# GateLoop attention and a gated feed-forward on one core: the results of two chunks in one group of quadrant matmuls

## The chip, the cores and the metric

One core of a Trainium2 chip. The metric is the device time of one execution in microseconds (us). Five engines work beside each other, each through its own instructions in program order: PE (TensorE, the matmuls; its weight loads are shown apart as PEld), DVE (VectorE), ACT (ScalarE), POOL (GpSimd) and SP (SyncE, which here only issues DMAs). Where one engine needs another's result, it waits on a semaphore.

## The reference

```python
# q, k, v, a_re, a_im: (B, H, S, D) = (4, 8, 768, 48)
mag = sqrt(a_re * a_re + a_im * a_im)
scale = minimum(mag, 0.999) / (mag + 1e-06)
a_re_n, a_im_n = a_re * scale, a_im * scale
for t in range(S):                       # S_re, S_im: (B, H, D, D), start at 0
    ar, ai = a_re_n[:, :, t, :, None], a_im_n[:, :, t, :, None]
    new_re = ar * S_re - ai * S_im
    new_im = ar * S_im + ai * S_re
    S_re, S_im = new_re + einsum('bhd,bhe->bhde', k[:, :, t], v[:, :, t]), new_im
    y[:, :, t] = einsum('bhd,bhde->bhe', q[:, :, t], S_re)
x = y.transpose(0, 2, 1, 3).reshape(3072, 384)
h = x @ w_in                             # w_in: (384, 2048)
g = h * erf(maximum(h, 0) + log1p(exp(-abs(h))))
out = g @ w_out                          # w_out: (2048, 384)
```

All of it is float32.

## The kernel before

**Units and chunks.** The 4 x 768 tokens are worked in 12 units of 256 tokens, three to a sequence, and each unit in two chunks of 128 tokens. A name such as 3.1 is unit 3, chunk 1. Instead of stepping through tokens, a chunk uses products of decays: keys and queries are scaled and turned by the running product of the complex gates, so that within a chunk the results are a masked product of queries, keys and values, and what came before the chunk is one state S per head. Real and imaginary parts stand side by side, so a head's key has 96 elements.

**The steps of a unit**, with the letters that the order below uses: gates are loaded (`g`, L803) and worked into angles and decays by ACT and DVE, with a running sum over tokens as a matmul (`m t o l r s a`, and `p`, whose sum is at L1040). k and q are loaded (`k`, `q`, L807) and v (`v`, L814). `K` and `Q` (`prep`) are each a DVE multiplication by the decay (L1064, kr or qr, in a small buffer named "part"), one by the turn (L1069, kt or qt) and, from unit 2 on, a DVE transpose of 32 x 32 blocks (L1075, into X). `M` (`move`) then puts the blocks in their places with 12 DMAs in four pieces (L1086), so that KQ holds keys and queries with the 96 elements on the partitions: 16 planes of 128 tokens, eight heads of keys and then eight of queries. Units 0 and 1 do this with matmuls and copies instead (`kT`, `qT`, L1093 and L1097). `A` (`scores`) makes for four heads at once the products of keys and queries (L1106, sc) and, on DVE, masks them (L1110, A). `S` (`state`) makes kv from keys and values (L1125), adds the old state (L1131, Skv) and scales (L1134). It writes the one of two state buffers that the chunk before last used. `Y` (`result`) makes a chunk's results. ACT copies them into xT (L1163).

**The quadrant matmuls.** The results of a chunk, transposed, are 384 x 128. `result` makes them in blocks of 32 output rows, with weights of 128 x 32 (values, times A) and 96 x 32 (state, times queries). Four blocks for four different quadrants of TensorE's columns are issued in turn. A chunk has 64 such matmuls, or 32 where there is no state yet (the first chunk of a sequence). In the profile they are the `y` rows of L1161. All other matmuls have 96 or 128 weight columns.

**The feed-forward.** `h` makes h from xT and w_in (L1174, hps, 12 matmuls with 256 columns a piece) and ACT copies it (L1177). `x` is the softplus on ACT (names z and yy), `e` is ACT's error function (e<-z) between four DVE operations (L1203 to L1209). `O` is the product with w_out: L1243 in units 0 to 2, and from unit 3 on seven products of halves instead of eight (L1267, results W, X, Y, Z, with sums of h and of the weights made by DVE, `f` and `b`). `u` steps at the start are matmuls that nobody reads, issued to keep PE busy (L1325, unread). `n`, `i` and `Z` load and look over the weights.

**Buffers.** Of PSUM, ps_b with two buffers is shared by the decay sums, kv and y; ps_a holds the scores, ps_h the hps and ps_o the results of `O`. KQ has one buffer, A two, "part" two, and k and q one each, for both chunks of a unit.

**The order.** Every step is a generator. A string, `ORDER`, written out by hand, names the steps one after another, and each name runs the step to its next `yield`. So `Y2.0` stands twice: its first place issues all matmuls of the group, its second the copy. The string therefore fixes what stands behind what in every engine's queue, SP's too, and where in PE's work each group comes. Activations whose functions lie in different tables have a table load between them on ACT (L787), so their number too follows from the order.

Of the kernel before, what the change touches and what calls it, by code (L numbers as in the profile page):

```python
# [10 lines left out]
FP = mybir.dt.float32  # L11
# [9 lines left out]
P = 128  # L21
# [28 lines left out]
u8_0 u4_38 u4_21 u4_20 u4_2 g0.0 u2_34 u2_41 u2_25 g0.0 g0.1 g0.1 H t0.0 t0.0 m0.0 m0.0 m0.0 m0.1 t0.0 m0.1 l0.0  # L50
l0.0 t0.1 l0.0 l0.0 m0.1 l0.0 t0.1 t0.1 p0.0 u8_1 n0 n0 l0.1 o0.1 l0.1 l0.1 l0.1 o0.0 l0.1 n0 n0 k0.0 q0.0 p0.0
p0.0 K0.0 u2_23 r0.0 a0.0 r0.1 a0.0 a0.0 Q0.0 p0.1 u2_22 a0.1 u2_40 u2_39 g1.0 n1 m1.0 n1 n1 s0.0 s0.0 s0.0 Q0.0
qT0.0.0 p0.1 q0.1 a0.1 t1.0 p0.1 p0.0 K0.0 kT0.0.0 kT0.0.1 qT0.0.1 Q0.1 a0.1 t1.0 qT0.0.0 s0.1 s0.1 s0.1 qT0.0.1
g1.0 kT0.0.0 k0.1 u2_24 v0.0 S0.0 n1 K0.1 kT0.0.1 t1.0 o1.0 r1.0 A0.0.0 A0.0.0 Q0.1 K0.1 p0.0 S0.0 A0.0.1 A0.0.1
n3 n3 g1.1 m1.0 m1.1 t1.1 g1.1 a1.0 m1.0 a1.0 t1.1 a1.0 t1.1 qT0.1.0 qT0.1.0 v0.1 S0.1 S0.1 p0.1 l1.0 n4 n2 m1.1
m1.1 l1.0 g2.0 g2.0 p0.1 kT0.1.1 kT0.1.1 qT0.1.1 qT0.1.1 l1.0 o1.1 l1.0 n3 l1.0 Y0.0 kT0.1.0 A0.1.1 A0.1.1
kT0.1.0 A0.1.0 A0.1.0 l1.1 Y0.0 l1.1 s1.0 l1.1 n3 p1.0 p1.0 q1.0 l1.1 n2 l1.1 n2 g2.1 g2.1 p1.0 p1.0 n5 n6 r1.1
Y0.1 v2.1 k1.0 Y0.1 Q1.0 n2 n4 n4 n4 s1.0 s1.0 Q1.0 p1.1 a1.1 t2 m2 m2 m2 h0.0.6 t2 t2 S0.1 o2 n6 n6 p1.1 h0.0.6
l2 a1.1 a1.1 l2 p1.1 l2 l2 l2 K1.0 K1.0 n7 p1.1 q1.1 n6 k1.1 K1.1 Q1.1 g3.1 h0.0.4 h0.0.4 v1.0 a2.0 r2 a2.0 n7
n7 n7 n5 n5 qT1.0.1 qT1.0.0 h0.0.0 qT1.0.1 h0.0.0 s1.1 qT1.0.0 h0.0.2 h0.0.2 s1.1 s1.1 p2.0 p2.0 kT1.0.1 h0.1.0  # L60
kT1.0.1 kT1.0.0 a2.0 h0.1.0 kT1.0.0 p2.0 x0.0 a2.0 x0.0 e0.0.0 e0.0.2 A1.0.1 A1.0.1 A1.0.0 n5 n8 A1.0.0 n8 a2.0
# [12 lines left out]
e0.1.6 e0.1.4 n13 g5.0 a4.1 K3.0 n14 a4.1 e0.1.4 n14 e0.1.6 n14 x1.0 h1.1.4 x1.0 O0.8 h2.1.2 p4.1 O0.9 h2.0.2
O0.11 p4.1 x1.0 p4.1 x1.0 S3.0 S3.0 K3.1 g5.1 g5.1 M3.0 M3.0 M3.0 M3.0 e1.0.0 e1.0.0 e1.0.0 e1.0.2 e1.0.2 h2.0.2
e1.0.0 e1.0.2 e1.0.0 e1.0.2 e1.0.2 h2.1.2 m5 m5 a4.1 a4.1 j m5 O0.13 O0.15 O0.15 e1.0.4 h2.0.6 h2.0.6 e1.0.6
e1.0.6 e1.0.4 e1.0.4 e1.0.4 a4.1 e1.0.6 e1.0.6 e1.0.4 h2.1.4 A3.0.1 K3.1 A3.0.1 Q3.1 e1.0.6 Q3.1 v3.1 A3.0.0 l5
O0.10 A3.0.0 t5 l5 t5 x1.1 l5 l5 x1.1 S3.1 O0.12 O0.14 O0.14 x1.1 h2.0.4 O1.1 O1.3 h2.1.4 Y3.0 t5 S3.1 l5 o5
S3.1 x1.1 l5 l5 e1.1.2 e1.1.0 e1.1.2 e1.1.2 e1.1.2 e1.1.0 e1.1.0 e1.1.2 s4 s4 s4 r5 k4.0 K4.0 e1.1.0 e1.1.0 K4.0
e1.1.6 e1.1.6 e1.1.4 e1.1.4 e1.1.6 e1.1.4 e1.1.6 e1.1.6 O1.5 h2.0.0 O1.0 O1.2 M3.1 M3.1 M3.1 M3.1 A3.1.0 A3.1.0  # L80
A3.1.1 A3.1.1 O1.7 e1.1.4 K4.0 q4.0 Q4.0 k4.1 K4.1 e1.1.4 h2.0.0 h2.0.4 x2.0 Y3.0 x2.0 x2.0 x2.0 v4.0 p4.1 a5.0
p4.0 h2.1.6 O1.9 O1.11 S4.0 Y3.1 h2.1.0 O0.14 a5.0 K4.1 Q4.0 Q4.0 S4.0 q4.1 Q4.1 e2.0.0 e2.0.0 e2.0.0 e2.0.2
e2.0.2 e2.0.2 e2.0.0 e2.0.0 e2.0.2 p5.1 p5.1 h2.1.0 p5.1 e2.0.2 e2.0.6 Y3.1 h2.1.6 e2.0.6 e2.0.6 e2.0.4 a5.0
a5.0 e2.0.4 e2.0.4 O1.4 O1.6 O1.8 O1.13 O1.10 p5.0 p5.0 a5.0 a5.0 a5.0 x2.1 p5.0 x2.1 e2.0.4 e2.0.6 e2.0.6
h3.0.2 p4.0 M4.0 M4.0 M4.0 q5.1 M4.0 O0.15 k5.0 g6.1 p5.0 a5.1 g6.0 a5.1 a5.1 a5.1 x2.1 t6 x2.1 A4.0.1 A4.0.1
S4.1 S4.0 A4.0.0 A4.0.0 K4.1 S4.1 Q4.1 e2.0.4 Q4.1 e2.1.2 e2.1.2 e2.1.2 h3.0.4 h3.0.4 a5.1 O1.12 e2.1.0 e2.1.0
e2.1.2 a5.1 a5.1 e2.1.0 e2.1.2 e2.1.0 e2.1.0 p4.1 k5.1 g6.0 g6.1 h3.0.2 Y4.0 Y4.0 O1.14 O1.14 m6 m6 s5 e2.1.4
O1.15 O1.15 e2.1.6 e2.1.4 e2.1.6 e2.1.4 e2.1.6 h3.0.0 h3.0.0 s5 s5 e2.1.4 e2.1.4 S4.1 m6 e2.1.6 e2.1.6 h3.0.6
h3.0.6 M4.1 M4.1 M4.1 M4.1 h3.1.0 x3.0 t6 h3.1.0 x3.0 l6 x3.0 l6 x3.0 A4.1.1 h3.1.4 O2.1 O2.3 l6 K5.0 K5.0 q5.0
Q5.0 Q5.0 e3.0.0 Q5.0 v5.0 h3.1.6 A4.1.0 S5.0 t6 Q5.1 K5.1 A4.1.1 Q5.1 A4.1.0 Y4.1 K5.0 o6 S5.0 e3.0.0 e3.0.2  # L90
e3.0.0 e3.0.0 e3.0.2 e3.0.2 e3.0.0 e3.0.2 h3.1.4 r6 l6 O2.5 O2.7 a6.0 e3.0.6 a6.0 l6 e3.0.2 h3.1.2 O2.0 h3.1.2
h3.1.6 O2.9 e3.0.4 e3.0.6 e3.0.6 e3.0.4 a6.0 a6.0 O2.2 M5.0 a6.0 e3.0.4 M5.0 M5.0 M5.0 O2.4 O2.6 A5.0.0 A5.0.1
l6 l6 a6.1 p5.0 v6.0 q6.0 e3.0.6 e3.0.6 b2 e3.0.4 x3.1 Y4.1 h4.0.0 x3.1 a6.1 a6.1 x3.1 A5.0.0 A5.0.1 a6.1 a6.1
Y5.0 a6.1 b0 x3.1 O1.14 K5.1 K5.1 S5.0 a6.1 e3.0.4 Y5.0 f3.0 b4 Q5.1 e3.1.0 e3.1.0 e3.1.0 e3.1.0 e3.1.0 e3.1.2
e3.1.2 e3.1.2 e3.1.2 e3.1.2 k6.0 v6.1 O2.11 O2.13 p6.0 p6.0 p6.0 h4.0.0 p6.1 p6.1 e3.1.6 e3.1.6 h4.0.2 h4.0.2
e3.1.4 Q6.0 e3.1.4 O1.15 e3.1.4 e3.1.6 g7.0 g7.0 g7.1 p6.1 K6.0 f3.0 g7.1 m7 m7 M5.1 m7 e3.1.6 e3.1.4 e3.1.6
M5.1 i0 k6.1 i1 p6.0 q6.1 p6.1 M5.1 M5.1 O2.15 h4.0.4 h4.0.4 t7 O2.8 O2.10 O2.15 t7 l7 O2.12 O2.14 O2.14 O2.15
O2.14 b2 b2 t7 b0 b0 i0 l7 s6 l7 l7 b4 l7 b6 b2 e3.1.4 i1 f3.1 b6 b6 b4 h4.0.6 h4.0.6 x4.0 x4.0 b4 f3.1 l7 l7
x4.0 h4.1.0 O3.0 h4.1.0 x4.0 e4.0.0 a7.0 b6 O3.1 e4.0.2 h4.1.6 h4.1.6 o7 O3.1 r7 s6 A5.1.1 A5.1.1 O3.2 O3.2
e4.0.0 e4.0.2 e4.0.0 e4.0.2 e4.0.0 e4.0.2 e4.0.2 b0 e4.0.0 A5.1.0 s6 e4.0.4 e4.0.6 A5.1.0 a7.0 a7.0 e4.0.4  # L100
e4.0.4 e4.0.6 e4.0.6 h4.1.4 h4.1.4 O3.3 O3.4 h4.1.2 O3.5 v5.1 Y5.1 O3.6 O3.7 h4.1.2 x4.1 Y5.1 x4.1 a7.0 e4.0.4
Q6.0 Q6.0 K6.1 e4.0.6 O3.5 O3.5 K6.0 K6.0 O3.5 e4.0.4 Q6.1 O3.4 O3.7 O3.7 p6.1 M6.0 M6.0 e4.0.6 a7.0 a7.0 a7.0
x4.1 x4.1 e4.1.0 e4.1.0 e4.1.0 e4.1.2 p7.1 h5.0.2 h5.0.4 O3.8 O3.9 O3.12 p7.0 O3.10 O3.13 O3.11 p7.1 h5.0.2 p7.1
e4.1.2 e4.1.0 e4.1.2 e4.1.0 e4.1.2 e4.1.2 e4.1.6 e4.1.4 e4.1.6 e4.1.6 e4.1.4 e4.1.4 M6.0 M6.0 a7.1 g8.1 p6.0
a7.1 e4.1.6 e4.1.4 p7.0 h5.0.4 p7.0 a7.1 O3.13 e4.1.6 a7.1 f4.0 e4.1.4 f4.1 O3.11 S6.0 h5.0.6 g8.0 t8 t8 h5.0.6
m8 h5.0.0 Q6.1 i2 i2 A6.0.1 a7.1 a7.1 f4.1 a7.1 S6.0 q7.1 p7.0 i3 A6.0.1 O4.0 O4.1 A6.0.0 O4.2 O4.1 i3 O3.11
h5.0.0 A6.0.0 g8.0 O4.3 p7.1 g8.1 q7.0 O3.13 f4.0 O4.2 t8 o8 Q6.1 K6.1 K6.1 M6.1 M6.1 M6.1 x5.0 x5.0 x5.0 m8
x5.0 O4.4 O4.4 e5.0.2 e5.0.0 e5.0.2 e5.0.0 Q7.0 e5.0.2 e5.0.2 e5.0.0 m8 e5.0.0 e5.0.2 e5.0.0 h5.1.6 h5.1.6 s7 s7
s7 Q7.0 h5.1.2 h5.1.2 e5.0.6 e5.0.6 e5.0.4 e5.0.4 S6.1 e5.0.4 l8 M6.1 v7.0 O4.5 O4.5 S6.1 e5.0.6 h5.1.0 h5.1.4
# [1342 lines left out]
```

## Time and profile before

| | |
|---|---|
| median of 3 runs | 659.39 us (659.02 to 659.49) |
| the profiled execution | 659.63 us |
| its span, first to last instruction | 657.9 us |
| granted TensorE clock, mean | 0.997 |
| y matmuls, values times A (L1161) | 768, 33.5 us busy |
| y matmuls, state times queries (L1161) | 640 |
| hps matmuls (L1174) | 1152, 260.7 us busy |
| DVE masks (L1110) | 48, 31.9 us busy |

The span is cut into engines' busy time, and the rows of the profile give groups of equal instructions: the busy time of the group, the mean length of one, and the idle time of the engine just before them with what ended it. Matmuls are pipelined: a row's length of one is longer than the time from one start to the next, so busy times of groups overlap. "PE y L1161" is TensorE's work at line 1161 on the tile y; "A <- B: 2.0, 3, 0.9" in the list of waits says that A waited for B 2.0 us in all, three times, 0.9 us at most.

### The profile page before, as it was taken

How to read it: one execution, taken by the hardware profiler on the slowest of the kernel's cores; microseconds unless marked ns; L12 is line 12 of the kernel's file. 1: busy time of each engine (PE TensorE's matmuls, PEld its weight loads, DVE VectorE, ACT ScalarE, POOL GpSimd, SP SyncE). 2: the span in 40 equal slices, each digit the busy share in tenths (PEclk: the TensorE clock that was granted, in tenths of full speed). 3: DMA queues.
4: the chain of work that ended last, by engine and by line, in shares of the span. 5: the costliest groups of instructions: out<-in, count | busy, mean ns of one | idle time of the engine just before them, and what ended most of it. 6: DMA issues, size and time to landing. Idle time of an engine off the chain costs nothing.

```text
span 657.9 us, 12296 instructions
## 1 busy us (share of the span) xinstructions
PE 642.2 (98%) x4728; PEld 562.6 (86%) x4728; DVE 599.2 (91%) x976; ACT 581.7 (88%) x765; POOL 1.1 (0%) x8
## 2 busy tenths in 40 slices
PE   8999999999999999999999999999999999999995
PEld 7778887777777778989999998999998999999985
DVE  6999999999979899999999899899999998877883
ACT  6999999999999999998998999998996894788730
POOL 0000000000000000000000000000000000000000
PEclk9999999999999999999999999999999999999998
DMA  8896886536254358137448525626626507410020
GB/s 212 221 239 160 191 205 111 119 63 108 37 110 73 49 117 188 22 48 193 73 73 193 97 43 141 120 50 145 121 49 122 132 14 187 90 25 24 1 73 27
DMA packets 282792, 70.19 MB, mean 107 GB/s; under 512 B 269396, under 2 KB 272488, under 8 KB 282728
## 3 DMA queue, kind: packets, MB, share of 16 engines
q1 hardware_dynamic: 282728, 69.36, 49.0%
q8 instruction: 38, 0.62, 0.4%
q14 instruction: 26, 0.21, 0.1%
HBM read 48.82 MB, written 4.75 MB: 81 GB/s over the span
## 4 chain that ended last, share of the span: by engine, by line
PE 48%; ACT 30%; DVE 15%; DMA 3%; issue 3%; SPq 1%; POOL 0%; DVEq 0%; POOLq 0%; ACTq 0%
PE hps L1174 21%; ACT L787 7%; ACT yy L788 5%; ACT z L788 5%; PE Y L1267 4%; PE Z L1267 4%; PE X L1267 3%; PE y L1161 3%; PE sc L1106 3%; ACT e L788 3%; DVE z L1203 3%; DVE yy L1205 3%; DVE e L1207 2%; PE W L1267 2%; PE kv L1125 2%
## 5 line engine op out<-in xcount | busy, mean ns | idle before, releaser
L1174 PE MATMUL hps<-xT,w_in_sb 128*128 128x256 f32 x1152 | 260.7, 380 | 0.4 <-ACT xT L1163 0.3
L1174 PEld LDWEIGHTS hps<-xT,w_in_sb 128*128 128x128 f32 x1152 | 216.1, 190 | 32.6 <-ACT h L1177 1.4
L787 ACT ACT_TABLE_LOAD x95 | 121.9, 1283 | 2.4 <-PEq L1436 0.9
L1203 DVE TENSOR_TENSOR z<-z,yy 128x512 f32<-128x512 f32 x96 | 64.5, 687 | 18.6 <-ACT e L788 18.0
L788 ACT ACTIVATE e<-z 128x512 f32<-128x512 f32 x96 | 57.8, 627 | 21.1 <-DVE h L1209 20.6
L1209 DVE SCALAR_TENSOR_TENSOR h<-e,h 128x512 f32<-128x512 f32 x96 | 65.0, 685 | 1.3
L1243 PE MATMUL ops<-w_out_sb,h 128*128 128x384 f32 x192 | 66.2, 488 | 0.0
L1205 DVE SCALAR_TENSOR_TENSOR yy<-z,yy 128x512 f32<-128x512 f32 x96 | 64.6, 688 | 1.6
L1207 DVE TENSOR_TENSOR e<-e,yy 128x512 f32<-128x512 f32 x96 | 64.6, 685 | 0.9
L1177 ACT COPY h<-hps 128x512 f32<-128x512 f32 x96 | 54.5, 577 | 8.4 <-PE hps L1174 8.3
L1243 PEld LDWEIGHTS ops<-w_out_sb,h 128*128 128x128 f32 x192 | 35.8, 190 | 21.7 <-issue 0.8
L1106 PEld LDWEIGHTS sc<-KQ 96*128 96x128 f32 x384 | 47.0, 192 | 4.7 <-ACT KQ L1097 1.8
L1106 PE MATMUL sc<-KQ 96*128 96x128 f32 x384 | 49.0, 277 | 1.3 <-ACT KQ L1097 1.0
L788 ACT ACTIVATE yy<-z 128x2048 f32<-128x2048 f32 (+1 forms) x25 | 46.1, 1842 | 0.8 <-DVE found L859 0.4
L788 ACT ACTIVATE z<-h 128x2048 f32<-128x2048 f32 (+1 forms) x25 | 46.1, 1844 | 0.6 <-ACT h L1177 0.3
L788 ACT ACTIVATE z<-z 128x2048 f32<-128x2048 f32 (+1 forms) x25 | 46.1, 1845 | 0.5
L788 ACT ACTIVATE yy<-yy 128x2048 f32<-128x2048 f32 (+1 forms) x25 | 46.0, 1842 | 0.3
L1161 PE MATMUL y<-A,v 128*32 128x128 f32 x768 | 33.5, 275 | 0.9 <-DVE Skv L1131 0.6
L1110 DVE TENSOR_TENSOR A<-sc,triu 128x512 f32<-128x512 f32 x48 | 31.9, 679 | 1.8 <-PE sc L1106 1.8
L1125 PEld LDWEIGHTS kv<-v,kt 128*96 128x96 f32 x320 | 29.8, 165 | 1.6 <-issue 0.7
L1125 PE MATMUL kv<-v,kt 128*96 128x48 f32 x320 | 29.8, 246 | 0.0
L1267 PE MATMUL Y<-T,S 128*128 128x192 f32 x144 | 26.5, 331 | 1.5 <-DVE out L1275 1.1
(122 smaller groups left out, 1054.7 us busy)
## 6 DMA issues: line engine op xcount, KB each, us to landing
KQ<-X SPq DMA_DIRECT2D x240, 64.0 KB
raw<-in_moe_w_in_dram SPq DMA_DIRECT2D x8, 768.0 KB
raw<-in_moe_w_out_dram SPq DMA_DIRECT2D x8, 768.0 KB
again<-in_moe_w_in_dram SPq DMA_DIRECT2D x8, 768.0 KB
ar<-in_a_re_dram SPq DMA_DIRECT2D x24, 192.0 KB
ai<-in_a_im_dram SPq DMA_DIRECT2D x24, 192.0 KB
k<-in_k_dram SPq DMA_DIRECT2D x24, 192.0 KB
q<-in_q_dram SPq DMA_DIRECT2D x24, 192.0 KB
```

The source lines that it names most:

```text
L787: scalar.preload_act_table_set(sets[0])
L788: scalar.activation(func=func, **kw)
L1106: nc.tensor.matmul(out=ps[:, j, :], lhsT=head("k", g * HG + j, u, c), rhs=head("q", g * HG + j, u, c), start=True, stop=True)
L1125: nc.tensor.matmul(out=kv[0:D2, j, :], lhsT=T["kt", u, c][:, j].rearrange("p u d -> p (u d)"), rhs=side(T["v", u][:, c, j // 2], j % 2), s ...
L1174: nc.tensor.matmul(out=ps[:, e, :], lhsT=w_in_sb[:, (sl * SLAB + i) // 2, kd, e * P:(e + 1) * P], rhs=T["xT", u][:, kd, :], start=(kd == 0 ...
L1177: scalar.copy(out=T["h", u, sl][:, i:i + 2, :], in_=ps)
L1203: vector.tensor_tensor(out=z, in0=z, in1=y, op=OP.mult)
L1205: vector.scalar_tensor_tensor(out=y, in0=z, scalar=-2.0, in1=y, op0=OP.add, op1=OP.mult)
L1207: vector.tensor_tensor(out=e, in0=e, in1=y, op=OP.mult)
L1209: vector.scalar_tensor_tensor(out=h, in0=e, scalar=1.0 / RT2, in1=h, op0=OP.add, op1=OP.mult)
L1243: nc.tensor.matmul(out=ps, lhsT=lhsT, rhs=w_out_sb[:, i, :], start=i == HALF, stop=i == KF - 1)
L1267: nc.tensor.matmul(out=ps, lhsT=a(sl)[:, i], rhs=b(sl, i), start=sl == 0 and i == 0, stop=sl == NSL - 1 and i == HALF - 1)
```

## The change

From unit 2 on (`APART`) `result` takes both chunks of a unit: one step `Y2` to `Y11` issues the 64 (or 32) matmuls of chunk 0 and then the 64 of chunk 1, into two tiles of ps_b, and its next two places make the two copies. Units 0 and 1 keep a step for each chunk. KQ has two buffers instead of one, and the masked scores are written over the key half of the chunk's KQ, four heads after the first or the last four scores are made, so the tile A goes. k and q are loaded into a tile for each chunk, one buffer each, where before the one buffer held both chunks of a unit. "part" has one buffer. And the string `ORDER` is another one: the same steps with the same number of places, but for the joined `Y` steps and the `u` steps at the start, stand in other places throughout.

The code:

```diff
@@ -804,7 +803,8 @@
             yield
 
     def load(nm, src, u, c):
-        nc.sync.dma_start(out=whole(ldq, nm, u, [P, C, H, D])[:, c], in_=rows(src, u, c))
+        t = T[nm, u, c] = ldq.tile([P, H, D], FP, tag=nm, name=nm)
+        nc.sync.dma_start(out=t, in_=rows(src, u, c))
         yield
 
     def load_v(u, c):
@@ -1060,8 +1060,8 @@
 
 
     def prep(nm, u, c):
-        a = att1.tile([P, H, D], FP, tag="part", name=nm + "r", bufs=2)
-        vector.tensor_tensor(out=a, in0=T[nm, u][:, c], op=OP.mult,
+        a = att1.tile([P, H, D], FP, tag="part", name=nm + "r")
+        vector.tensor_tensor(out=a, in0=T[nm, u, c], op=OP.mult,
                              in1=T["pr", u][:, c, "qk".index(nm), :].rearrange("p (h d) -> p h d", d=D))
         yield
         t = T[nm + "t", u, c] = att1.tile([P, H, 2, D], FP, tag=nm + "t", name=nm + "t")
@@ -1076,7 +1076,7 @@
             yield
 
     def columns(u, c):
-        return whole(att2, "KQ", (u, c), [P, 2 * H, P], bufs=1)
+        return whole(att2, "KQ", (u, c), [P, 2 * H, P])
 
     def move(u, c):
         kq, x = columns(u, c), T["X", (u, c)]
@@ -1106,7 +1106,7 @@
             nc.tensor.matmul(out=ps[:, j, :], lhsT=head("k", g * HG + j, u, c), rhs=head("q", g * HG + j, u, c),
                              start=True, stop=True)
         yield
-        A = T["A", u, c, g] = att2.tile([P, HG, P], FP, tag="A", name="A")
+        A = T["A", u, c, g] = columns(u, c)[:, g * HG:(g + 1) * HG]
         vector.tensor_tensor(out=A, in0=ps, in1=triu.unsqueeze(1).to_broadcast([P, HG, P]), op=OP.mult)
         yield
 
@@ -1127,41 +1127,45 @@
         yield
         t = kv[0:D2]
         if not first:
-            t = att1.tile([P, H, D], FP, tag="part", name="Skv", bufs=2)[0:D2]
+            t = att1.tile([P, H, D], FP, tag="part", name="Skv")[0:D2]
             vector.tensor_tensor(out=paired(t), in0=paired(kv[0:D2]), in1=sides(sbuf[(u * C + c - 1) % 2]), op=OP.add)
             yield
         w = T["w", u, c][0:D2].unsqueeze(2).to_broadcast([D2, H, D])
         vector.tensor_tensor(out=sides(sbuf[(u * C + c) % 2]), in0=paired(t), in1=paired(w), op=OP.mult)
         yield
 
-    def result(u, c):
-
-        first = u % PER == 0 and c == 0
-        S = sbuf[(u * C + c - 1) % 2]
+    def result(u, chunks):
+
         x = whole(xp, "xT", u, [P, KD, NT])
-        ps = ps_b.tile([P, KD, P], FP, tag="b", name="y")
-
-        steps = [[] for _ in range(P // QUAD)]
-        for i in range(KD):
-            for b in range(P // QUAD):
-                pair, o = divmod((i * P + b * QUAD) // QUAD, 2 * D // QUAD)
-
-                parts = [(0, o * QUAD)] if o * QUAD < D else []
-                parts += [(1, o * QUAD + GAP)] if (o + 1) * QUAD > D else []
-                todo = []
-                for e, lo in parts:
-                    g, k_ = divmod(2 * pair + e, HG)
-                    both = [(T["v", u][:, c, pair, lo:lo + QUAD], T["A", u, c, g][:, k_, :])]
-                    if not first:
-                        both.append((S[0:D2, pair, lo:lo + QUAD], head("q", 2 * pair + e, u, c)))
-                    todo += both[::-1] if (len(steps[b]) + len(todo)) % 4 else both
-                steps[b] += [(i, lhsT, rhs, n == 0, n == len(todo) - 1) for n, (lhsT, rhs) in enumerate(todo)]
-        for turn in zip(*steps):
-            for b, (i, lhsT, rhs, start, stop) in enumerate(turn):
-                nc.tensor.matmul(out=ps[b * QUAD:(b + 1) * QUAD, i, :], lhsT=lhsT, rhs=rhs, start=start, stop=stop)
-        yield
-        scalar.copy(out=x[:, :, c * P:(c + 1) * P], in_=ps)
-        yield
+        out = []
+        for c in chunks:
+            first = u % PER == 0 and c == 0
+            S = sbuf[(u * C + c - 1) % 2]
+            ps = ps_b.tile([P, KD, P], FP, tag="b", name="y")
+            out.append((c, ps))
+
+            steps = [[] for _ in range(P // QUAD)]
+            for i in range(KD):
+                for b in range(P // QUAD):
+                    pair, o = divmod((i * P + b * QUAD) // QUAD, 2 * D // QUAD)
+
+                    parts = [(0, o * QUAD)] if o * QUAD < D else []
+                    parts += [(1, o * QUAD + GAP)] if (o + 1) * QUAD > D else []
+                    todo = []
+                    for e, lo in parts:
+                        g, k_ = divmod(2 * pair + e, HG)
+                        both = [(T["v", u][:, c, pair, lo:lo + QUAD], T["A", u, c, g][:, k_, :])]
+                        if not first:
+                            both.append((S[0:D2, pair, lo:lo + QUAD], head("q", 2 * pair + e, u, c)))
+                        todo += both[::-1] if (len(steps[b]) + len(todo)) % 4 else both
+                    steps[b] += [(i, lhsT, rhs, n == 0, n == len(todo) - 1) for n, (lhsT, rhs) in enumerate(todo)]
+            for turn in zip(*steps):
+                for b, (i, lhsT, rhs, start, stop) in enumerate(turn):
+                    nc.tensor.matmul(out=ps[b * QUAD:(b + 1) * QUAD, i, :], lhsT=lhsT, rhs=rhs, start=start, stop=stop)
+        yield
+        for c, ps in out:
+            scalar.copy(out=x[:, :, c * P:(c + 1) * P], in_=ps)
+            yield
 
 
     def ff_in(u, sl, i):
@@ -1222,7 +1226,7 @@
         vector.tensor_tensor(out=A21, in0=A11, in1=A21, op=OP.subtract)
         yield
 
-    PLAIN = 3
+    PLAIN, APART = 3, 2
     T["T4"] = const.tile([P, HALF, HD], FP, name="T4")
 
     def bank(u, nm):
@@ -1352,6 +1356,8 @@
         steps[f"b{r}"] = sums_of_weights(r, 2)
     for u in range(NU):
         plain = u < PLAIN
+        for nm, chunks in [(f"{u}.{c}", [c]) for c in range(C)] if u < APART else [(f"{u}", range(C))]:
+            steps["Y" + nm] = result(u, chunks)
         for c in range(C):
             at = f"{u}.{c}"
             steps["g" + at] = load_gates(u, c)
@@ -1367,7 +1373,6 @@
                 steps["S" + at] = state(u, c)
             for g in range(NHG):
                 steps[f"A{at}.{g}"] = scores(u, c, g)
-            steps["Y" + at] = result(u, c)
             steps["a" + at], steps["p" + at] = g_angle(u, c), g_decay(u, c)
         for at, cc in [(f"{u}.{c}", (c, c + 1)) for c in range(C)] if u < 2 else [(f"{u}", ALL)]:
             for nm, f in (("m", g_mag), ("t", g_tan), ("o", g_off), ("l", g_log), ("r", g_turn), ("s", g_sin)):
```

`ORDER` is replaced as a whole. The places around the results of unit 2 (a line "..." leaves out the rest):

```diff
-e0.0.6 e0.0.4 e0.0.6 m4 e0.0.6 e0.0.4 n15 k3.1 h1.0.4 h1.0.4 s3 h1.0.6 h1.0.6 Y2.0 p2.0 q3.0 p3.1 n12 e0.0.6
-S2.0 n12 M2.1 M2.1 M2.1 M2.1 n13 p3.0 v3.0 s3 p3.0 p3.1 s3 l4 x0.1 Y2.0 l4 x0.1 l4 x0.1 h1.1.6 h1.1.6 x0.1
...
-A2.1.0 A2.1.0 A2.1.1 A2.1.1 l4 e0.1.2 e0.1.0 e0.1.2 e0.1.0 h1.1.4 e0.1.2 e0.1.0 e0.1.2 e0.1.0 a4.0 a4.0 n14 Y2.1
-v4.1 Y2.1 g5.0 e0.1.6 e0.1.6 e0.1.6 e0.1.4 e0.1.4 e0.1.4 n13 Q3.0 n13 p4.0 O0.5 O0.7 p4.0 a4.0 a4.0 p4.0 a4.0
...
+A2.0.1 t4 n15 l4 O0.1 O0.0 O0.2 O0.4 O0.6 O0.3 A2.1.0 A2.1.0 A2.1.1 A2.1.1 e0.1.2 o4 l4 K3.0 e0.1.2 e0.1.0
+e0.1.0 h1.0.6 r4 h1.1.4 h1.1.4 e0.1.2 Y2 Y2 Y2 a4.0 v3.0 e0.1.0 e0.1.2 a4.0 e0.1.0 e0.1.2 e0.1.0 e0.1.6 e0.1.6
```

## The prediction, made before the changed kernel was run

> **What bounds it now.** I read the busy table first, then the same table by stretches of 100 us (the columns after each window: its length, PE, PEld, DVE, ACT and POOL busy, the granted clock, DMA's share, GB/s), then the list of waits, the costliest groups, and last the TensorE rows around one result group.
>
> ```profile
> PE 642.2 (98%) x4728; PEld 562.6 (86%) x4728; DVE 599.2 (91%) x976; ACT 581.7 (88%) x765; POOL 1.1 (0%) x8
> ```
>
> ```profile
> 0.00:100.00 100.00, 95.53 (x813) 81.32 (x814) 92.98 (x159) 93.82 (x159) 1.09 (x8) 1.00 0.84 203
> ...
> 200.00:300.00 100.00, 98.69 (x660) 83.10 (x659) 95.18 (x153) 98.81 (x126) 0.00 (x0) 1.00 0.43 83
> ...
> 500.00:600.00 100.00, 100.00 (x787) 92.63 (x786) 88.29 (x143) 76.02 (x92) 0.00 (x0) 1.00 0.39 87
> ```
>
> PE is busy all the time, so only what PE does, or how long it is idle, can move the end. But up to 300 us ACT is as full as PE (98.81 against 98.69), and DVE is near. From 400 on ACT has room. Work taken from PE early can therefore turn into waiting for ACT; taken late it should be won. The clock is 1.00, so time is not lost there.
>
> "Busy" overlaps, so I work with pitches, start to start: an hps matmul 216 ns, a product of ff_out 162, scores 112, kv 85, y 27. By them PE's work adds up to some 640 us and its true idle time to some 11: about 7 in the first 40 us, 1.0 at 182, 0.8 at 193, 1.1 at 281, small ones, and 2.6 behind 630.
>
> **The term that the change aims at.** Before, each of the 24 result groups stands alone between full-size matmuls. TensorE's rows around one (start, length, what, count):
>
> ```profile
> 487.23 1.46 PE L1267 MATMUL W<-w_out_sb,h 128*128 128x192 f32 x8
> 488.62 0.43 PE L1161 MATMUL y<-A,v 128*32 128x128 f32 x8
> ...
> 490.18 0.40 PE L1161 MATMUL y<-A,v 128*32 128x128 f32 x8
> 490.52 1.57 PE L1267 MATMUL W<-w_out_sb,h 128*128 128x192 f32 x8
> ```
>
> The eighth W starts at 487.23 + 7 x 0.162 = 488.37; one pitch on would be 488.53, and y starts at 488.62: 0.09 lost going in. The last y starts at 490.18 + 0.40 - 0.27 (one y's own length) = 490.31; W follows at 490.52, 0.21 later instead of a y pitch of 0.03: 0.18 lost coming out. And those eight W take 1.57 instead of 1.46: 0.11 more, which is the gap behind the first. 0.38; other neighbours (hps: 309 instead of 216 going in, 200 and 320 instead of 216 coming out; kv: 178 instead of 85) give 0.36 to 0.37. I take 0.37. Within a group, the seams where A and KQ take turns cost nothing (64 matmuls in 1.69 us), so I take the seam between the two chunks, same quadrant shape, as free. Ten pairs are merged (units 2 to 11): 10 x 0.37 = **-3.7 us on PE**. The work in the groups is the same. If the seam drained too, the term would be 0.
>
> **What the merge ties together.** Both chunks' scores, masks (DVE, 0.68 us each) and the first chunk's state must now be there before the group, and both accumulators are taken at once, which are all the two buffers that sums, kv and y share. The next sum or kv waits for the first copy xT<-y (ACT, 0.46 long at 482.28), which stands in ACT's queue behind any softplus step (1.84 us an activation). After the groups of units 8 and 9 the next such user is a few pieces behind. State of the second chunk must come behind the group, as it overwrites the S that the first chunk reads. In before the group often starts 0.14 to 3 us after its last mask, so there was little slack to give.
>
> I walked both hand-written orders with the durations above, and asked, for each PE step, how much ACT and DVE work must be done before it, against PE work before it. In before the tightest places stand at 0. In after ACT is late by 2.8 us at 85, 2.5 at 176, 2.3 at 303 and 3.8 at 350 (the hps of unit 6, whose buffer ACT frees), DVE by 2.8 at 101 and 2.1 at 207. These aren't added: one idle stretch of PE serves all later ones. The start gives up to 1.2 back: the first decay sum comes behind 20 warm matmuls, not 30, and this wait may go:
>
> ```profile
> ACT e L788 <- DVE h L1209: 20.6, 15, 2.9
> DVE z L1203 <- ACT e L788: 18.0, 23, 4.2
> ...
> SPq L1086 <- DVE X L1075: 115.1, 13, 16.6
> ...
> ACT pr L788 <- PE sum L1040: 1.2, 1, 1.2
> ```
>
> (In each row: the total, how often, the longest.) The first two rows say that ACT and DVE already pass blocks to and fro with no reserve. Net, PE's idle time by 350 us grows from 6.6 to about 9.3: 3.8 - 1.2 = 2.6, **between 0 and +3.8; I take +2.2**, as lateness at one place was partly idle time elsewhere before.
>
> **The moves.** With two KQ buffers a chunk's keys and queries needn't wait for the last group that read the only buffer (SPq L1086 on PE y: 1.9 us in all), so nothing is lost there. But the new order puts some moves nearer to their scores:
>
> ```profile
> L1086 SPq DMA_DIRECT2D KQ<-X x240: 586/627/1604, 75.1 to 576.4; - x120
> ```
>
> Twelve issues of 0.63 are 7.5 us of SP's queue; the last lands about 2.2 after it began (first issue 541.7, last 549.0, landed 551.2): near 10 us from X to scores, and more where SP has other transfers in between. In before the shortest stretch between X and scores is 10.2. In after, laid on before's times, it is 6.7 for chunk 3.1 (near 150), 7.0 for 9.1 (near 471), 8.5 for 10.1 (near 518), the rest 9 and more. That would be up to 3.3, 3.0 and 1.5 us of PE waiting. What stands behind sc on PE is the next hps or product, in order, so nothing slips past. If PE falls behind at any place before, DVE and SP gain the same time, so part is the idle time counted above (3.1). **0 to +4.5 late; I take +0.9.** What is late next is the mask A, then the group.
>
> **Loads by chunk.** k and q now have one buffer each that holds one chunk, so a load waits for the previous chunk's prep rather than the previous unit's. From buffer release to use there are 5.1 us (k10.1), 5.9 (k8.1), 6.8 (q2.1) and more; the loads in before take 2.5 to 5, one 8.5, from issue to landing. A late one stops DVE, behind which z, yy, e, h stand, for perhaps 1 us; DVE is 88% busy by 500 us. **0 to +2; I take +0.2.** A rule speaks against this part: the Trainium skill, "DMA: Bandwidth & Descriptors", section "Rules for kernel authors", says to issue a DMA early and wait on its semaphore late. The rule names no price; the trace gives one chain piece of that kind (k, 4.63 us at 251.5).
>
> **ACT's tables.** Where neighbouring functions lie in different tables, a load stands between them:
>
> ```profile
> L787 ACT ACT_TABLE_LOAD x95 | 121.9, 1283 | 2.4 <-PEq L1436 0.9
> ```
>
> The same walk that gives 95 for before gives 98 for after: 3 x 1.283 = 3.85 us of ACT, all at 480 to 520 us, where ACT is idle 8 to 24% of the time: 0, at most 3.85. I take 0. The Trainium skill, "ScalarE: Activation LUTs", section "What ACT_TABLE_LOAD costs", puts a drain of about 1.38 us beside the load; here the next activation starts at 480.66, 0.02 after the load of 479.36 ends, so no such drain shows, and the page's estimate of 8.0 us is not used.
>
> **Scores in place of keys, one "part" buffer.** The mask writes the same 128 x 512 elsewhere; DVE alone uses "part", in order: 0, and up to 0.3 if the mask's place makes it wait for the last score (it waits for that already).
>
> **The tail.** Behind the last hps PE has 34.0 us of work before and 31.4 after, and ACT 16.1 against 12.6 behind its last h copy, as the last softplus is begun on half a tile earlier. The tail's stalls (1.29 at 631, four of 0.3 to 0.5) shrink: **0 to -2.6; I take -2.0.**
>
> **Sum.** -3.7 + 2.2 + 0.9 + 0.2 - 2.0 = -2.4, and the start's 1.2 is in the 2.2. The profiled execution: span 657.9, so 655.5; 659.63 in all, so 657.2; the median shown is 0.24 lower: about **657.0**. Ends of all terms together: -6.3 and +10.6, but they exclude one another in part, since PE idle anywhere serves ACT, DVE and SP.
>
> **Rivals.** (a) *The stalls are absorbed*: the order's places hide them as before's do, only 0 to +1 is left; -3.7 - 2 + 0.7 = -5.0: **654.4**. For it: PE 100.00 from 500 on. Against: ACT 98.81 up to 300. (b) *ACT takes it back*: up to 300-350 us the saving of some four merges turns into waiting for ACT, and the coupling uses up the tail: within 1 us of before, **659**. For it: the first two waits above. (c) *Slower*: the moves decide. If the three short stretches cost their 3.3 + 3.0 + 1.5 in full, the merge's 3.7 is overtaken, and the lag of ACT at 350 (2.6) comes on top: -3.7 + 7.8 + 2.6 - 2.0 = +4.7; with half the move waits +0.8 to +2: **661**. It decides from the point where the windows' waits are over some 3.5 us. Against: DVE finishes X earlier if PE is late. (d) *The seam drains*: term 0, then +1.3: 660.7; little speaks for it.
>
> **Chances.** The forecast (655.5 to 658) 0.37, (a) 0.24, (b) 0.19, (c) 0.16, (d) 0.04. Faster by more than 0.2% (1.3 us, about what a measurement of this kernel can tell): forecast, (a) and a little of (b): 0.64; within it 0.15, slower 0.21. The range, 653.0 to 661.2, leaves out the ends of (a) and (c); the forecast's own is 655.5 to 658.
>
> **What would show it.** Right: PE busy down to about 639; y rows with 128 and 0.03 pitch through the middle, ten fewer drains; PE waits "sc <- DMA KQ" of a few tenths to 1 us near 150, 471 and 518; ACT above 98% to 350. Wrong: a gap of 0.2 in the middle of a y group (d); "sum" or "kv" waiting for xT in rows over 1 us, or sc waiting 3 us at a time (c); tail stalls unchanged.

## The result: no change that can be measured

| | before | after |
|---|---|---|
| median | 659.49 us (13 runs) | 659.41 us (13 runs) |
| ratio | | 1.0002, 95% interval 0.9995 to 1.001 |
| span of the profiled execution | 657.9 us | 657.6 us |

Nine of the changed kernel's thirteen executions, with a granted clock of 0.997 or more, took 659.1 to 659.5 us (median 659.23), the other four, at 0.995 and 0.996, 660.2 to 660.7; the last section says what the traces show of that.

The profile after, busy times and tables:

```profile
PE 640.9 (97%) x4728; PEld 564.0 (86%) x4728; DVE 598.3 (91%) x976; ACT 583.8 (89%) x768; POOL 1.1 (0%) x8
...
L786 ACT ACT_TABLE_LOAD x98 | 125.7, 1283 | 2.5 <-PEq L1441 0.9
```

The groups did get cheaper. TensorE's rows around the group of unit 9, which now holds both chunks (96 matmuls):

```profile
479.39 1.30 PE L1164 MATMUL y<-KQ,v 128*32 128x128 f32 x40
480.50 0.62 PE L1164 MATMUL y<-KQ,S 96*32 96x128 f32 x16
...
481.82 0.40 PE L1164 MATMUL y<-KQ,v 128*32 128x128 f32 x8
482.15 1.57 PE L1271 MATMUL Z<-T,h 128*128 128x192 f32 x8
```

The 96 matmuls start within 2.56 us (the last at 481.82 + 0.40 - 0.27 = 481.95), 27 ns apart, and the seam between the chunks shows no gap. What is lost going in and out, counted as in the prediction over all groups, fell from 8.65 to 4.60 us: 4.05 us. There are 13 groups instead of 24, one fewer than counted, because the new order also puts the two steps of unit 1 next to each other.

So 4 us of TensorE's time are gone, and the end stands where it stood. The same stretches as before (length, PE, PEld, DVE, ACT, POOL busy, clock, DMA's share, GB/s), with one more:

```profile
0.00:100.00 100.00, 94.35 (x750) 80.86 (x751) 94.58 (x162) 94.44 (x159) 1.09 (x8) 1.00 0.85 203
200.00:300.00 100.00, 98.82 (x734) 84.00 (x733) 93.56 (x151) 99.12 (x124) 0.00 (x0) 1.00 0.43 83
500.00:600.00 100.00, 99.71 (x785) 92.10 (x784) 87.49 (x143) 76.01 (x93) 0.00 (x0) 1.00 0.41 89
...
100.00:200.00 100.00, 99.85 (x647) 75.40 (x646) 93.74 (x144) 98.83 (x127) 0.00 (x0) 1.00 0.51 95
```

ACT is still full from 100 to 300 us. Behind 500 us, where TensorE had 100.00, it now has 99.71: it waits again. And stretches of 100 us hide what ACT does behind 400. Between 480 and 500 us it was idle for 2.5 us in the kernel before (first row) and is full in the changed one (second row); between 520 and 540 us it was busy for 17.23 us and is now for 19.79 (third row):

```profile
480.00:500.00 20.00, 20.00 (x180) 18.78 (x179) 19.53 (x30) 17.48 (x21) 0.00 (x0) 1.00 0.33 54
480.00:500.00 20.00, 20.00 (x198) 18.95 (x187) 18.73 (x27) 19.76 (x25) 0.00 (x0) 1.00 0.24 44
520.00:540.00 20.00, 19.71 (x240) 18.26 (x239) 18.62 (x31) 19.79 (x22) 0.00 (x0) 1.00 0.33 64
```

Two of TensorE's waits, its rows around the scores of 5.1 and of 9.1:

```profile
256.16 1.06 PE L1106 MATMUL sc<-KQ 96*128 96x128 f32 x8
258.24 1.13 PE L1106 MATMUL sc<-KQ 96*128 96x128 f32 x8 [1.02 <-DVE qt L1069]
...
471.49 1.46 PE L1271 MATMUL Y<-w_out_sb,h 128*128 128x192 f32 x8
473.54 1.13 PE L1106 MATMUL sc<-KQ 96*128 96x128 f32 x8 [0.59 <-DMA wrow<-pr]
```

The releasers named there had long been done. The DMAs of the moves landed at 258.0 and 473.4, just ahead of each second score.

To see where the 4 us went I lined the traces up by TensorE's work still to do, in pitches and without the switches, and took the difference of the times at which equal work is left. Positive is earlier than the changed kernel, in us, at its times:

| kernel | 97 | 199 | 342 | 465 | 486 | 526 | 588 |
|---|---|---|---|---|---|---|---|
| before | +1.9 | +0.2 | -0.3 | -0.7 | -0.1 | -0.1 | -0.1 |
| split_early | -1.5 | -1.5 | -1.6 | -1.6 | -1.5 | -2.1 | -2.2 |
| split_late | -0.1 | -0.1 | -0.2 | -0.4 | -0.9 | -1.7 | -1.7 |
| late_fix | 0.0 | 0.0 | 0.0 | -0.9 | -0.4 | -1.2 | -2.1 |
| tweak | -0.5 | -0.5 | -0.5 | -0.8 | -0.2 | -0.8 | -0.8 |

The first row compares two different orders, so it moves by some 0.4 us from one place to the next. It tells three things. Up to 97 us the changed kernel falls behind on TensorE by 1.9, and that doesn't matter: ACT's idle time up to 100 us is 5.6 us instead of 6.2, and by 199 the lag is down to 0.2. From there to 465 us the changed kernel gains 0.9. Between 465 and 526 it loses 0.6 again, although two more merges, of units 9 and 10, fall there. Between DVE's last instruction and the end 5.0 to 6.1 us pass in these traces, so a row doesn't end at the difference of the spans.

### The profile page after: what moved, and what is told of

It is laid out like the page before. It is cut to its first block, busy times and chain, and to the rows that moved or that the text cites. A ratio compares the mean times of both kernels' runs of the same rounds, so it can differ in the third digit from the quotient of the medians.

```text
span 657.6 us, 12344 instructions
## 1 busy us (share of the span) xinstructions
PE 640.9 (97%) x4728; PEld 564.0 (86%) x4728; DVE 598.3 (91%) x976; ACT 583.8 (89%) x768; POOL 1.1 (0%) x8
## 4 chain that ended last, share of the span: by engine, by line
ACT 40%; PE 28%; DVE 21%; issue 5%; DMA 3%; SPq 2%; DVEq 0%; ACTq 0%
PE hps L1178 13%; ACT L786 10%; ACT yy L787 7%; ACT z L787 6%; ACT e L787 4%; PE Y L1271 3%; ACT CS L787 2%; DVE yy L1209 2%; DVE z L1207 2%; PE X L1271 2%; DVE h L1213 2%; DVE e L1211 2%; ACT y L787 2%; PE Z L1271 2%; PE sc L1106 2%
## 5 line engine op out<-in xcount | busy, mean ns | idle before, releaser
L1110 DVE TENSOR_TENSOR KQ<-sc,triu 128x512 f32<-128x512 f32 x48 | 32.2, 682 | 0.8 <-PE sc L1106 0.8
L1164 PE MATMUL y<-KQ,v 128*32 128x128 f32 x768 | 31.5, 274 | 0.0
L1271 PE MATMUL X<-T,S 128*128 128x192 f32 x144 | 25.4, 327 | 1.2 <-DVE S L1282 1.2
```

What stands on the lines that cost most here:

```text
L1271: nc.tensor.matmul(out=ps, lhsT=a(sl)[:, i], rhs=b(sl, i), start=sl == 0 and i == 0, stop=sl == NSL - 1 and i == HALF - 1)
```

## The experiments

The medians are each of 11 or 12 runs (5 for hoist, 4 for before_more_late); the kernel before, run in turn with them, had 659.2 to 659.5. The changed kernel was not run again beside them, so a difference to it of a few tenths says little.

**Early groups taken apart again** (split_early).

```diff
+    APARTS = (2, 3, 4, 5)
-... if u < APART else ...
+... if u < APART or u in APARTS else ...
-h1.1.4 h1.1.4 e0.1.2 Y2 Y2 Y2
+Y2.0 h1.1.4 h1.1.4 e0.1.2 Y2.1 Y2.0 Y2.1
```

> The changed kernel with the groups of units 2 to 5 taken apart again: chunk 0's group stands one TensorE step earlier, so each unit has two more switches (4 x 0.37 = 1.5 us of TensorE time in the first 275 us). If ACT sets the pace there (theory A: the saving of the early merges was never worth anything): 0 to +0.4 us against the changed kernel. If TensorE sets it (theory B: a merge is worth 0.37 us anywhere and the loss is elsewhere, in the start for one): +1.5 us.

660.36 us, ratio to before 1.0008 (0.9998 to 1.0019). The median is 0.95 above the changed kernel's. In the profiled execution 1.5 us were lost before the first of these groups, when ACT waited for a sum:

```profile
42.92 0.58 ACT L781 ACTIVATE F<-sum,column 128x384 f32<-128x384 f32 x1 [1.02 <-PE sum L1013]
```

The sum was late because TensorE ran slower there: the granted clock from 39 to 42 us is 0.50 in this run. Eight of its matmuls ahead of that sum, in the changed kernel and in this run:

```profile
38.84 1.04 PE L1093 MATMUL tr<-ident,qt 128*96 128x128 f32 x8
...
38.95 1.92 PE L1087 MATMUL tr<-ident,qt 128*96 128x128 f32 x8
```

The edit has no part in that, as the order is the same up to there. From 97 to 342 us, with the four groups taken apart, it lost 0.1 us more, for 1.5 us of switches, and its seven executions at a granted clock of 0.997 or more have a median of 659.43, 0.2 above the changed kernel's nine. That is in the range of theory A: early on TensorE's time is worth next to nothing. The executions of one kernel spread by 1.6 us (659.1 to 660.7 for the changed one), and this one shows a 1 us difference of ACT's at 42 us kept to the end: a difference of 1 us between medians is little here, and I read the traces.

**Late groups taken apart again** (split_late): the same with `APARTS = (6, 7, 8, 9, 10, 11)`.

> The same for units 6 to 11: 6 x 0.37 = 2.2 us of TensorE time from 325 us on. Theory A: the late merges' saving is eaten by TensorE's waits for scores, kv and sums of the new order (2.4 us more than before between 380 and 600), which the extra switches partly fill: +0.5 to +1.2 us. Theory B: +2.2 us.

660.24 us, 1.0008 (0.9999 to 1.0017), +0.8 on the changed kernel, as theory A said; in the trace, of an execution 0.9 us above the median, it falls from -0.2 at 342 to -1.7 for 2.2 us of switches. So a late merge is probably worth something in this order, by the medians over a third of its price, more than an early one.

**The waiting steps moved behind the next ready one** (late_fix).

```diff
-A9.1.0 A9.1.0 O7.5 O7.7 A9.1.1 e8.0.4 A9.1.1
+O7.5 O7.7 A9.1.0 A9.1.0 A9.1.1 e8.0.4 A9.1.1
...
-A5.1.1 O3.0 O3.1 O3.2
+O3.0 O3.1 A5.1.1 O3.2
```

The scores of 10.1 go behind O8.2, the kv of 8.0 behind O6.3, that of 11.0 behind O8.8.

> The changed kernel with five matmul steps moved behind the next ready step, where TensorE waits for them: the scores of 5.1 (1.19 us of waiting at 257), 9.1 (0.75 at 473) and 10.1 (0.38 at 521), the kv of 8.0 (0.34 at 405) and of 11.0 (0.36 at 537). Theory A: the waits behind 340 us are on the path and come back, that at 257 doesn't, as ACT is full there: -1.2 to -1.8 us. Theory B: all come back, -3.0 us. If the waits only stand for a lag of ACT or DVE (theory C: they are as full late as early), 0 to -0.3 us, with the waits found again a step later.

660.46 us, 1.0012 (1.0002 to 1.0022): slower by 1.0, where theories A and B had it faster and C nearly the same. The trace (its code lines stand six lower) shows the wait at 257 gone, and found again 37 us on:

```profile
259.66 1.05 PE L1100 MATMUL sc<-KQ 96*128 96x128 f32 x8
...
293.02 1.46 PE L1265 MATMUL W<-w_out_sb,h 128*128 128x192 f32 x8
294.88 1.13 PE L1100 MATMUL sc<-KQ 96*128 96x128 f32 x8 [0.40 <-DMA KQ<-X]
```

Ahead by 1.3 at 261, it is level at 302. Behind 400 us the kv and scores put later made later ones wait (0.46 at 426, 0.48 at 523, 0.85 at 544). A wait that is eased here is paid at a later one, as theory C had it: no single one of these places holds the time.

**Less work for TensorE early** (cut_pe_early).

```diff
-            for i in (i0, i0 + 1):
+            for i in ((i0,) if u == 1 and jj == 0 and i0 in (6, 0, 2, 8, 10) else (i0, i0 + 1)):
```

> The changed kernel with 5 of the 32 matmuls of unit 1's product with w_out for chunk 0 left out (so its rows of the output lack 5 of 16 parts): 3.2 us less for TensorE, between 125 and 235 us. Theory A: 0 to -0.8 us, TensorE's idle time before 340 us grows by the rest. Theory B: -3.2 us.

658.76 us, 0.999 (0.9979 to 1.0001): -0.65 of 3.2, in the range of theory A. TensorE's busy time in this stretch falls, ACT's stays at the same 98.83:

```profile
100.00:200.00 100.00, 97.38 (x637) 73.39 (x636) 94.00 (x144) 98.83 (x126) 0.00 (x0) 1.00 0.52 95
```

and one wait of TensorE, which the changed kernel doesn't have, takes most of what is left:

```profile
PEld sum L921 <- ACT pr L787: 1.8, 1, 1.8
```

By 179 us the whole 3.2 us are gone.

**Less work for ACT early** (cut_act_early).

```diff
-        act(out=z, in_=z, func=AF.Ln, bias=1.0)
+        few = slice(0, 1 if u == 2 else None)
+        act(out=z[:, few], in_=z[:, few], func=AF.Ln, bias=1.0)
```

> The changed kernel with one of the four activations of unit 2's softplus done on an eighth of its columns, twice (unit 2's rows are wrong by it): 3.2 us less for ACT near 200 and 230 us. If ACT paces the kernel up to 340 us: -1.5 to -3 us, as TensorE has some 3 us of idle time to give between 200 and 340. If not: 0.

658.18 us, 0.9984 (0.9972 to 0.9995): -1.2 on the changed kernel, less than expected if ACT alone set the pace, but the only gain whose interval leaves out 1. In the trace it leads by 1.5 at 261, 1.2 at 465 and 0.1 at 526: it lost the rest at the scores of 10.1, which waited 1.46 us instead of 0.36, because their move landed at 520.7 where the changed kernel has 520.9. So ACT's time is worth something early, and the gain meets a limit late.

**Less work for TensorE late, twice** (cut_pe_late with unit 7, cut_pe_last with unit 8 and five other steps, the last line).

```diff
+        LESS = (("X", 0, 0), ("X", 0, 1), ("W", 0, 0), ("W", 0, 1), ("Z", 1, 0))
-                for i in range(HALF):
+                for i in ((0, HALF - 1) if u == 7 and (nm, c, sl) in LESS else range(HALF)):
...
+        LESS = (("Z", 1, 0), ("Z", 1, 1), ("Z", 0, 0), ("W", 0, 0), ("W", 0, 1))
```

> The changed kernel with 5 of the 14 product steps of unit 7 halved (10 of 56 matmuls left out, so unit 7's output is incomplete): 3.25 us less for TensorE between 400 and 480 us. If TensorE sets the pace there: -3 us. If what holds the kernel between 470 and 540 us is the chain of gate work, moves and scores of units 9 and 10 (theory A as it now stands, after moving the waiting steps gave no gain): -0.5 to -1.5 us, with the waits for the scores of 9.1 and 10.1 longer by the rest.

658.8 us, 0.9993 (0.9982 to 1.0004), -0.6: between 465 and 506 us the trace loses all of the 3.25 us, in waits of 0.6 at 465, 1.1 at 473 (scores of 9.1) and 1.2 at 497, for one of ACT's copies of h:

```profile
PE hps L1178 <- ACT h L1181: 1.1, 1, 1.1
```

So TensorE doesn't set the pace at 440 to 500 us either.

> The changed kernel with 5 of the 14 product steps of unit 8 halved, all between 539 and 552 us (unit 8's output is incomplete): the same 3.25 us less for TensorE as in the run on unit 7, 70 us later. The chain of waits is TensorE's alone from 538 to 596 us, so TensorE should pace the kernel here: -2.2 to -3.2 us against the changed kernel. If the tail's chain on ACT (from 598 us) doesn't follow TensorE: 0 to -1.

661.29 us, 1.002 (1.0005 to 1.0035): slower by 1.9 with less to do. The chain of waits had named TensorE alone there, and that misled me. In the trace, with the work gone, it caught up with ACT, waited 2 us for a copy of h, and then ran half as fast:

```profile
545.90 0.81 PE L1272 MATMUL W<-w_out_sb,h 128*128 128x192 f32 x4
548.75 4.54 PE L1178 MATMUL hps<-xT,w_in_sb 128*128 128x256 f32 x12 [2.03 <-ACT h L1181]
```

Twelve hps take 2.75 us elsewhere. The granted clock between 546 and 553 us was 0.76. That and the wait cost more than the 3.25 us. The twelve executions show how often: four have a granted clock of 0.997 and took 658.8 to 659.4 us, eight have 0.991 to 0.996 and took 660.0 to 662.7. The four have a median of 659.07, 0.2 under the changed kernel's nine: the answer that had 0 to -1. TensorE doesn't set the pace here either.

**Less work for ACT at the end** (cut_act_tail): as cut_act_early, with `(u, sl) == (11, 0)`.

> The changed kernel with one of the four activations of the softplus of unit 11's first half done on an eighth of its columns (unit 11's rows are wrong by it): 1.6 us less for ACT at 600 us. If ACT's chain from 598 to 630 us sets the end in the changed kernel as in the one before (and the earlier start of the last softplus is worth nothing for that reason): -1.0 to -1.6 us. If TensorE's remaining work sets it, as the prediction's term for the tail supposed: 0 to -0.3.

659.19 us, 0.9997 (0.9987 to 1.0007): -0.2, the size of the second answer, but not for its reason alone. In the changed kernel the chain ran through ACT from 598 to 630 us; with ACT eased it runs through TensorE. Of the chain of this run:

```profile
628.87 1.31 PE W L1272 x8
...
636.76 2.87 PE Y L1272 x16
```

TensorE's W ends at 630.18; in the changed kernel ACT's last error function ended at 630.75. The product Y behind both starts at 636.76 instead of 637.06: two chains, 0.3 us apart.

**Moves and transposes put earlier** (hoist).

```diff
-M9.1 M9.1 M9.1 M9.1 p10.1 g11.0
+p10.1 g11.0
...
+M9.1 M9.1 M9.1 M9.1 g11.1
...
-M10.0 M10.0 M10.0 i10 i11 Q10.1 K10.1
+M10.1 M10.1 M10.1 M10.1 i10 i11
```

The three pieces of M10.0 follow its first one, Q10.1 and K10.1 go ahead of a11.0, K9.1 and Q9.1 to either side of Q9.1's second place.

> The changed kernel with the KQ moves of 9.1, 10.0 and 10.1 and the transposes in front of them put earlier in the queues of SP and DVE (SP stands idle at 492 to 496 us behind a transfer of unit 11's gates, with three pieces of 10.0's move queued behind it). Theory A: the scores of 9.1 and 10.1 no longer wait (0.75 and 0.36 us), and what hangs on them behind 521 us comes sooner: -1.0 to -2.0 us against the changed kernel. Theory C (ACT and DVE lag anyway): 0 to +0.5, as each transpose put forward delays a step of the feed-forward by 0.95 us.

675.8 us, 1.0252 (1.023 to 1.0274): 16 us slower, which neither theory had. On SP's queue the moves now stood ahead of a load of q and of two readings of the weights, and DVE stood still for those, with ACT and TensorE behind it:

```profile
DVE found L859 <- DMA again<-in_moe_w_out_dram: 9.4, 2, 9.1
ACT z L787 <- DVE found L859: 8.4, 1, 8.4
...
DVE qr L1064 <- DMA q<-in_q_dram: 6.9, 1, 6.9
```

**More switches in the kernel before** (before_more_late).

```diff
-        for turn in zip(*steps):
+        for n, turn in enumerate(zip(*steps)):
+            if u in APART and 2 * n == len(steps[0]): yield
```

> The kernel before with 11 of the 12 result groups of units 6 to 11 cut in two, another TensorE step between the halves: 11 more switches, 4.1 us more for TensorE from 325 us on. The chain of before is TensorE's alone behind 405 us: +3.0 to +4.1 us (+0.27 to +0.37 for each). If the gate work and moves pace before too: +1 to +2 us.

669.24 us, 1.0151 (1.0131 to 1.0172): far over both, and no price of a switch. Half the groups had their first half put ahead of an earlier step, and these waited for their own data (1.5 us at 406, 1.9 at 511, 1.2 and 1.0 behind 586). Behind the wait at 511 the granted clock was 0.50 as well, from 514 to 517 us. One part can be read: up to 404 us, four groups cut (1.5 us of switches) cost 0.4 us.

**Two places mended** (tweak).

```diff
-A9.1.0 A9.1.0 O7.5 O7.7 A9.1.1
+O7.5 O7.7 A9.1.0 A9.1.0 A9.1.1
...
-A10.0.1 a11.1 M10.1 M10.1 a11.1 O7.13 f8.0 e8.1.4 f8.1
+A10.0.1 a11.1 M10.1 M10.1 O7.13 f8.0 e8.1.4 f8.1 a11.1
```

> The changed kernel with two places of its order mended: the scores of 9.1 one product later (0.75 us of waiting at 473 us), and DVE's step that waits 2.2 us at 514 us for a small transfer of unit 11's gates put behind three steps of the feed-forward. If the waits between 470 and 540 us are a lag of these chains that can be filled: -0.5 to -1.2 us against the changed kernel. If the lag is only found again a step later, as when five steps were moved: -0.2 to +0.8.

660.16 us, 1.0003 (0.9992 to 1.0015), as the second answer had it. Both waits are gone or short (DVE's 2.2 us is 0.66), TensorE gained 0.5 us at 473, and by 506 it had lost them again.

**Two readings of the weights left out** (no_look).

```diff
+        if i in (10, 11): yield; yield; return
```

> The changed kernel without the second reading of two of the 16 parts of the weights (part of the check on the inputs; the output itself is the same): two transfers of 768 KB and 2.0 us of SP's queue between the moves of 10.0 and 10.1, and two DVE steps of 0.93 us at 510 to 514 us. If SP's queue and DVE hold the kernel between 500 and 540 us (the move of 10.1 takes 12 us instead of the 9.7 that twelve transfers need): -0.8 to -2.0 us against the changed kernel. If ACT, DVE, SP and TensorE are so close there that easing one only shows the next (as the cuts on TensorE say): 0 to -0.5 us.

659.74 us, 1.0007 (0.9997 to 1.0017): no gain. DVE's freed time became waiting. DVE's row of a step of the gates of unit 11, in the changed kernel:

```profile
516.56 0.55 DVE L1002 SCALAR_TENSOR_TENSOR th<-s,th 1x384 f32<-1x384 f32 x1 [2.19 <-DMA s<-F]
```

The same row in no_look, where the wait in brackets is 2.1 us longer:

```profile
516.76 0.55 DVE L1002 SCALAR_TENSOR_TENSOR th<-s,th 1x384 f32<-1x384 f32 x1 [4.28 <-DMA s<-F]
```

What it waits for stands on SP's queue between the pieces of 10.1's move. SP's rows in the changed kernel, with no gap from 508.9 on:

```profile
508.91 2.00 SPq L1086 DMA_DIRECT2D KQ<-X  x3
511.01 0.43 SPq L1053 DMA_DIRECT2D wrow<-pr  x1
511.48 1.93 SPq L1086 DMA_DIRECT2D KQ<-X  x3
513.53 0.57 SPq L999 DMA_DIRECT2D s<-F  x1
514.15 5.14 SPq L1086 DMA_DIRECT2D KQ<-X  x6
```

The move can't start before the DVE transposes at 508.8 and its last DMA lands at 520.9. With the two readings gone it starts and lands at the same times; its first DMAs in no_look:

```profile
508.86 1.93 SPq L1086 DMA_DIRECT2D KQ<-X  x3
```

That holds the scores of 10.1 and, through s<-F, the gates of unit 11. It is the one late place where the runs show what a step waits for. What would move it as a whole wasn't found.

## Why the prediction was right and wrong

The forecast, 657.0 us, was wrong by 2.4; the time lies in the range and is that of rival (b), 659, at 0.19. One term makes most of the miss: -2.0 for the tail, where 0.3 came. Up to 584 us the sum had -0.4 and the traces show about -0.1, and that is partly luck: the switches and the early half came out a little better than forecast, the late half worse. Rival (b) has the right time and, for the first half, the right reason; behind 350 us and for the tail it has not.

- **The switches: right.** -3.7 forecast, -4.05 measured, the seam free; rival (d) is out.
- **ACT takes it back (+2.2 up to 350 us): right in size, and in kind as far as tested.** Up to 342 us six groups fewer save 2.2 us, and the changed kernel is ahead by 0.3, so 1.9 are taken back. An early merge is worth next to nothing: 3.2 us less for TensorE gained 0.65, four groups taken apart cost 0.1 in the trace. At the start ACT's wait for the sum at L1040 is off the list, as foreseen, and ACT is 0.6 us ahead at 100 us.
- **The moves (+0.9, 0 to +4.5): the place partly right, the size and the reason not.** TensorE waits for the scores of 9.1 (0.75 us), 10.1 (0.36) and 7.1 (0.31); near 150 us (3.1) nothing shows, and 5.1, which I had not named, waits 1.19 us. From 342 to 584 us five groups fewer save 1.8 us, and the lead goes from 0.3 to 0.1: some 2 us are lost, against 0.9 for the moves and 0.2 for the loads. It is not the moves' own 1.4 us alone: easing single waits (late_fix, tweak, no_look) gave nothing. So the step that failed here is the assumption that PE at 100% paces the kernel behind 400 us and that ACT has room there. Two cuts of 3.25 us on TensorE gained 0.6 and 0.2, and in the changed order ACT is busy 99% of the time from 460 to 500 and from 520 to 540 us.
- **The loads (+0.2): right.** No wait for k or q is on DVE's list.
- **The tables (0, at most +3.85): the count right, the price open.** 98 loads, three more, and 2.1 us more ACT time (583.8 instead of 581.7). But the idle 8 to 24% of ACT, for which I took 0, is that of the kernel before in stretches of 100 us. In the changed kernel twelve loads instead of nine start between 460 and 540 us, 3 x 1.283 = 3.85 us more, where ACT is nearly full. They may be what uses up the late half; no run tried it.
- **The tail (-2.0): wrong.** From 584 to 631 us the two traces are within 0.1 us of each other. One of TensorE's products behind the last error function, before and after, starts 0.4 us earlier, and the spans end 0.3 us apart:

```profile
637.47 1.57 PE L1267 MATMUL Y<-T,S 128*128 128x192 f32 x8 [0.36 <-DVE S L1220]
...
637.06 1.57 PE L1271 MATMUL Y<-T,S 128*128 128x192 f32 x8 [0.37 <-DVE S L1224]
```

I had counted each engine's work behind the last hps and taken the difference for a gain. There are two chains of almost equal length, ACT's and TensorE's, and cut_act_tail shows that 1.6 us less of one moves the end by 0.3.

## What to carry to other kernels

Where three engines are each 89 to 97% full, the share of busy time names no bound: take a few us of work from one engine and see whether the end moves, before pricing a saving on it. Room on an engine is read from stretches as short as the place where it is needed, and in the new order, not the old one. A saving on an engine that only just leads is given back at the next wait for another, so price it up to that wait. In a queue that runs in order, putting a transfer earlier is putting everything behind it later.

## What was not expected of the hardware

After TensorE had stood for 2.2 us at 546 us in cut_pe_last, seven of twelve hps came 0.43 instead of 0.216 us apart (clock 0.76 between 546 and 553). In hoist it stood for 6.7 us, and the next products took twice their time. The window of hoist behind that wait (granted clock 0.53, third figure from the end):

```profile
529.00:535.00 6.00, 5.74 (x20) 5.74 (x21) 5.67 (x11) 5.97 (x6) 0.00 (x0) 0.53 0.45 87
```

TensorE's rows of hoist on both sides of it, eight products each, 1.46 us ahead and 2.93 us behind:

```profile
521.10 1.46 PE L1271 MATMUL X<-w_out_sb,h 128*128 128x192 f32 x8
529.26 2.93 PE L1271 MATMUL Y<-T,S 128*128 128x192 f32 x8 [6.70 <-DVE S L1224]
```

"TensorE: Matmul & The Clock Gate" of the Trainium skill, in Part 1, "What's actually happening", has the clock halved after an idle stretch of about 3.4 us. The 6.7 us of hoist agree with it, at 0.53; the 2.2 us of cut_pe_last (a wait of 0.66 us lay 3 us ahead of them) are shorter, and there the measurement decides.

Still less was enough near 38 us. There TensorE stands for 1.2 us in the changed order (its rows have 1.05 for it), where the kernel before stands for 0.3, and two of the traces kept, split_early and cut_pe_late, have half the clock behind it, 0.50 and 0.54 from 39 to 42 us. The others have the same stand and no such stretch. The traces' own records of the clock tell them apart: the stretches between two changes of the clock are whole multiples of 3.41 us (34.13 and 614.4 in split_early, 648.53 in the changed kernel), as if it were set on a beat of that length. In the two, a beat ends at 38.8 and 38.3 us, just behind the stand; in the others at 37.0 to 37.7 or at 39.5 to 39.7. So it would be chance which executions lose the time. The stand alone isn't enough: the kernel before stands 1.1 us at 24 us and keeps its clock, and what else it takes no run shows. In the changed kernel four of thirteen have a clock of 0.995 or 0.996 and took 1.1 us longer than the other nine; they have no trace, so that they lose it near 38 us is likely, not shown. Of 101 executions of the kernel before, run beside the experiments, none is under 0.997.
